# One attention and FFN kernel, its instruction order searched anew: slack behind every DMA, the first batch's k in single PSUM banks, part of v on GpSimd, other token tiles, the last tile by column halves

## The chip, the cores and the metric

The kernel runs on one core of one Trainium2 chip. The core has five engines that run their own instruction streams and wait for each other by semaphores: TensorE (PE, matmuls; PEld is its weight load), VectorE (DVE), ScalarE (ACT), GpSimd (POOL) and SyncE (SP, which here only issues DMAs). The metric is the device time in microseconds (us) of one execution; smaller is better. The profile is of one execution and covers its span, from the first instruction to the last.

## The reference

Linear attention with an exponential feature map in 8 batches of 8 heads, 576 tokens and head size 64, and then a feed-forward network (FFN) with squared ReLU on all 4608 tokens.

```python
def phi(x):
    proj = np.einsum('bhsd,df->bhsf', x, w_phi)              # 64 -> 128
    proj = proj - np.max(np.abs(proj), axis=-1, keepdims=True)
    return np.concatenate([np.exp(proj), np.exp(-proj)], axis=-1)
q_p, k_p = (phi(q), phi(k))
kv = np.einsum('bhsf,bhsd->bhfd', k_p, v)
z = np.sum(k_p, axis=2)
num = np.einsum('bhsf,bhfd->bhsd', q_p, kv)
den = np.einsum('bhsf,bhf->bhs', q_p, z)[..., None] + 1e-06
attn_out = num / den
x = attn_out.transpose(0, 2, 1, 3).reshape(4608, 512)
h = np.maximum(x @ w_in, 0.0)                                # 512 -> 2048
out = h * h @ w_out                                          # 2048 -> 512
```

All inputs and the output are float32 in DRAM; the kernel computes its matmuls in bfloat16.

## The kernel before

**Loads.** POOL issues all loads of q, k, v, w_in (`win`, four tiles of 512 KB) and w_out (`wout`, four tiles); they are cast to bfloat16 on the way. A batch of k, q or v is 512 tokens in one or more DMAs of 128 to 512 KB (`load`, line 446, and `load_q`, line 465) and a tail of 64 tokens in two small ones (line 454). SP issues the stores of the output (line 926) and the DMA transposes: of batches 2 to 7 the whole k and q into `kT` and `qT` (line 532, 18 blocks of 128x128), and of batches 1 to 7 the attention's result `xo` into `xT` (line 793), since the FFN needs it with features on partitions. In batches 0 and 1 PE transposes k and q itself (line 519, copied out of PSUM in lines 524 and 526), and in batch 0 also `xo` (line 782).

**Attention of a batch.** k comes in five groups: 0 to 3 of four 128-token blocks and 4 for the tail. `kgroup_ops` projects a group by w_phi (line 548) into a pair of PSUM banks, one for each half e of the partitions; the matmuls are 64 rows deep, two at a time on the two halves of PE. DVE takes the largest magnitude (`mk`, line 567), then ACT takes both exponentials of the pair (`kp` and `kn`, line 576, 1024 columns each). The subtraction of the maximum is not made on k: `em_ops` takes exp(-mk) and exp(mk) (lines 588 and 595), and `v_ops` multiplies v by them into `va` (DVE, lines 610 and 614, two products for each group or pair of groups). `kv_ops` sums kp with va (lines 628 and 633), and ACT copies the result to `kv` (line 642). q is projected twice: with tokens on partitions for the maxima (`qmax_ops`, lines 548 and 660, DVE 667, and `en` = exp(-2 mq), ACT 674) and with features on partitions for the exponentials (`q_ops`, PE 702, ACT 717). `out_ops` makes the numerators and denominators: matmuls NA, a product by `en` on DVE (line 744), matmuls NB on top (line 732), then reciprocal (752) and product (756) into `xo`.

**FFN.** The 4608 tokens are nine chunks of 512. Chunk 0 is done in sixteen groups of 16 matmuls of 128 columns (`ffn_in_small`, line 885), so that it can begin with the first 128 tokens. Chunks 1 to 8 are done by `ffn_in` in sixteen groups of four 512-column matmuls (line 874), each followed by ReLU on ACT (857) and the square on DVE (863). `ffn_out` (line 912) takes sixteen groups of four 512-column matmuls for each chunk, four groups to a tile of 128 tokens, then ACT copies the tile to `ot` (line 920) and SP stores it. Chunks are consecutive in blocks of 64 tokens: `blk_of` gives nine blocks to a batch, so chunk c takes blocks 8c to 8c+7, which lie in two batches. Batches with odd numbers have their tail in front, those with even numbers at the end. `xT` has three buffers for the chunks.

**The order.** All of this is first recorded in `Plan` as operations, each with an engine, an assumed cost, a due time (`key`) and what it reads and writes. `Machine` then plays the operations on a model of the engines, the PSUM banks and the DMA queues, and so fixes the order of the instructions of each engine; the instructions are written out in that order and pinned to it. An engine takes the ready operation with the earliest key. The keys come from a few constants in `K` and, for batches 0 and 1, from a table of single keys, `K["B"]`. `LIM` limits the open PSUM buffers of a kind (`tp` transposes, `att` attention pairs, and so on). An operation with a `release` time also waits for an ACT instruction that the model has finished by then; in this way loads are held back. A DMA's end in the model is its transfer and a fixed time after it:

```python
def dma_settle(t):
    for at, o in self.dma_advance(t):
        o.done = at + (SW_OUT if o.eng == "POOL" else HW_OUT)
```

While PE would have nothing to do in the first 23 us of the model, filler matmuls on a tile of zeros (`warm`, line 991) are put in.

Of the kernel before, what the change touches and what calls it, by code (L numbers as in the profile page):

```python
# [20 lines left out]
SW_IN, SW_OUT, HW_IN, HW_OUT = 1.5, 1.3, 0.75, 0.95  # L21
BEGIN = {"POOL": 1.25}
# [3 lines left out]
def act_cost(n):  # L26
    return n / 1200 + 0.050, n / 1200 + 0.165 + SEM
# [10 lines left out]
class Op:  # L38
    __slots__ = ("eng", "occ", "lat", "key", "fn", "opens", "closes", "dma", "tiled", "release", "gate",
                 "succ", "n", "ready", "at", "seq", "what", "ins", "left", "done")  # L40

    def __init__(self, eng, cost, key, fn, opens, closes, dma, tiled, release, seq, what):
        self.eng, (self.occ, self.lat), self.key, self.fn = eng, cost, key, fn
        self.opens, self.closes, self.dma, self.seq, self.what = opens, closes, dma, seq, what
        self.tiled, self.release, self.gate, self.ins = tiled, release, None, None
        self.succ, self.n, self.ready, self.at, self.done = {}, 0, 0.0, None, None

# [47 lines left out]
class Machine:  # L95
# [34 lines left out]


# [24 lines left out]
    def run(self):  # L156
# [28 lines left out]
        def dma_settle(t):  # L185
            for at, o in self.dma_advance(t):
                o.done = at + (SW_OUT if o.eng == "POOL" else HW_OUT)
                for s in o.succ:
                    released(s, o.done)
                post(o.done, o.eng)  # L190
# [6 lines left out]
        def pick(name, e, t):  # L197
# [7 lines left out]
            if mode:  # L205
                for i, op in enumerate(A):
                    if op.tiled and op.key <= t + self.ahead:
                        b = self.place(op.opens, t + 1e-9)
                        if b is not None:
                            op.opens.base = b  # L210
                            return A.pop(i)
# [4 lines left out]
            for i, op in enumerate(A):  # L216
                if op.tiled and not go and t < op.key + self.patience:
                    if op.key <= t:
                        tight = True
                    if fallback is None and self.place(op.opens, t + 1e-9) is not None:  # L220
                        fallback = i
                    continue
                if op.opens is not None:
                    b = self.place(op.opens, t + 1e-9, tight and op.opens.size == 1)
                    if b is None:
                        if op.key <= t:
                            tight = True
                        continue
                    op.opens.base = b
                return A.pop(i)  # L230
            if fallback is not None:
                op = A.pop(fallback)
                op.opens.base = self.place(op.opens, t + 1e-9)
# [3 lines left out]
        while left:  # L237
# [47 lines left out]
            if op.opens is not None:  # L285
                g = op.opens
# [22 lines left out]
def kernel(  # L309
# [67 lines left out]
    NQP = 3  # L377
    qp, qn = ring("qp", NQP, [8 * P]), ring("qn", NQP, [8 * P])
    xo = ring("xo", 3, [8 * D])
    rden = ring("rden", 3, [8], F32)  # L380
    xT = [ring(f"xT{c}", 2, [4, 2, P]) for c in range(3)]
    hr = ring("hr", 4, [TCH])
    h2 = [ring(f"h2{c}_", 4, [4, TCH]) for c in range(2)]
    ot = ring("ot", 3, [DM], F32)

# [21 lines left out]


# [16 lines left out]
    add("DVE", dve_cost(32), -20, f_warm, w=["warm"], what="warm")  # L425

    for b in range(2):
        for sg in range(2):
            def fn(b=b, sg=sg):
                pin(nc.vector.memset(va[b][sg][:, 32:40, :], 0.0))  # L430
            add("DVE", dve_cost(260), -11 if b == 0 else 0.0, fn, w=[("ve", b, sg, 4)], what="zero")
# [9 lines left out]
    def load(src, dst, b, key, tag, prs=((0, 4),), single=True, release=0.0):  # L441

        x = dst[b % 2]
        for a, z in prs:
            def fn(a=a, z=z):
# [4 lines left out]
                dma=(LD["main"] * (z - a) / 4, SW_IN, "ld"), release=release, what=tag)  # L450
        if single:
            for hi in range(2):
# [4 lines left out]
                ladd(b, (0.72, 0), key + 0.01, fn, w=[(tag, b % 2, "s", hi)], dma=(LD["s"], SW_IN, "ld"),  # L457
                    release=release, what=tag + "s")

    def load_q(b, key, jjs=(0, 1), single=True, release=0.0):  # L460

        x = xq[b % 2]
        for jj in jjs:
# [4 lines left out]
            ladd(b, (0.72, 0), key, fn, w=[("xq", b % 2, jj)], dma=(LD["main"] / 2, SW_IN, "ld"), release=release, what="xq")  # L468
        if single:
            load(q, xq, b, key, "xq", prs=(), release=release)  # L470

# [3 lines left out]
    def load_win(i, key):  # L475
# [3 lines left out]
        ladd(None, (0.72, 0), key, fn, w=[("win", i)], dma=(LD["w"], SW_IN, "ld"), what="win")  # L479

    def load_wout(i, key):
# [3 lines left out]
        ladd(None, (0.72, 0), key, fn, w=[("wout", i)], dma=(LD["w"], SW_IN, "ld"), what="wout")  # L485
# [7 lines left out]
    def blk_of(b, c):  # L493

        if c == 4:
            return b * NB + (0 if b % 2 else 8)
        return b * NB + (1 if b % 2 else 0) + 2 * c

    def attention(b):
        s2 = b % 2  # L500
        pe_in = b in PE_IN
        pe_x = b in PE_X
# [552 lines left out]
```

## Time and profile before

| What | us |
|---|---|
| median of 3 runs (lowest, highest) | 378.27 (376.19, 507.98) |
| the profiled execution's own time | 377.19 |
| its span | 375.4 |

| Group (line, engine) | count | mean ns | busy us |
|---|---|---|---|
| FFN-out matmuls, 512 columns (912, PE) | 536 of 576 recorded | 379 | 137.7 |
| FFN-in matmuls, 512 columns (874, PE) | 512 | 382 | 130.3 |
| ReLU, 512 columns (857, ACT) | 144 | 602 | 85.2 |
| square, 512 columns (863, DVE) | 144 | 418 | 59.3 |
| exponentials of k, 1024 columns, kp and kn (576, ACT) | 64 | 1020 and 1029 | 32.5 and 32.9 |
| exponentials of k, 512 columns, kp and kn (576, ACT) | 16 | 596 and 586 | 4.8 and 4.7 |
| maxima of k, 1024 columns (567, DVE) | 32 | 1216 | 38.6 |
| maxima of k, 512 columns (567, DVE) | 8 | 685 | 5.5 |
| products with v, 512 columns (610, DVE) | 16 | 688 | 10.8 |

| DMA | count | KB each | median us from issue to landing |
|---|---|---|---|
| store of a tile | 32 | 256 | 2.3 |
| store of half a tile | 8 | 128 | 2.8 |
| transpose of xo into xT | 50 | | 2.4 |
| transpose of a batch's k, q | 6, 6 | | 4.8, 5.8 |
| load of v, of k | 8, 7 | 512 | 6.4, 8.4 |
| load of win, of wout | 4, 4 | 512 | 12.0, 14.2 |

A matmul's mean is its latency, not its share of PE: successive matmuls overlap, and a group of four wide ones takes less than four times its mean. In the table "busy" is the union of the instructions' times. "Idle before" in the profile is time in which an engine had nothing, and what ended it is named after the arrow. A line of the chain of waits, "start, us, what", is a piece of the path that ended last, followed back from the end.

### The profile page before, as it was taken

How to read it: one execution, taken by the hardware profiler on the slowest of the kernel's cores; microseconds unless marked ns; L12 is line 12 of the kernel's file. 1: busy time of each engine (PE TensorE's matmuls, PEld its weight loads, DVE VectorE, ACT ScalarE, POOL GpSimd, SP SyncE). 2: the span in 40 equal slices, each digit the busy share in tenths (PEclk: the TensorE clock that was granted, in tenths of full speed). 3: DMA queues.
4: the chain of work that ended last, by engine and by line, in shares of the span. 5: the costliest groups of instructions: out<-in, count | busy, mean ns of one | idle time of the engine just before them, and what ended most of it. 6: DMA issues, size and time to landing. Idle time of an engine off the chain costs nothing.

```text
span 375.4 us, 8607 instructions
## 1 busy us (share of the span) xinstructions
PE 353.5 (94%) x3459; PEld 200.2 (53%) x3499; DVE 250.1 (67%) x417; ACT 270.1 (72%) x504; POOL 66.3 (18%) x96
## 2 busy tenths in 40 slices
PE   8997899968999999999999988999899999999995
PEld 7876768624554555455455544554445544444442
DVE  4888798883888877887678685876688762222200
ACT  2988998786798868889678977777889774444321
POOL 8634161052002500250016000610000000000000
PEclk9999999998999999999999999999999999999999
DMA  8999999699934992399519932995120222001022
GB/s 94 195 200 204 149 112 148 122 119 141 137 71 91 146 192 64 59 152 205 86 48 129 203 73 73 115 196 111 43 71 9 47 61 70 30 28 56 30 58 82
DMA packets 101799, 39.62 MB, mean 106 GB/s; under 512 B 76544, under 2 KB 97152, under 8 KB 101760
## 3 DMA queue, kind: packets, MB, share of 16 engines
q0 software_dynamic: 50592, 18.36, 43.4%
q1 hardware_dynamic: 51168, 20.72, 25.0%
q8 instruction: 27, 0.44, 0.5%
q14 instruction: 12, 0.10, 0.1%
HBM read 36.77 MB, written 9.44 MB: 123 GB/s over the span
## 4 chain that ended last, share of the span: by engine, by line
PE 70%; ACT 13%; DVE 7%; DMA 6%; issue 3%; ACTq 0%; DVEq 0%; SPq 0%; POOLq 0%
PE psum L912 25%; PE psum L874 24%; PE psum L732 5%; DMA xT<-xo 4%; PE psum L548 4%; ACT kn L576 4%; ACT hr L857 3%; PE psum L628 3%; PE psum L885 3%; ACT kp L576 3%; PE psum L702 2%; DVE va L614 2%; DVE mk L567 2%; DMA xk<-in_k_dram 1%; PE psum L991 1%
## 5 line engine op out<-in xcount | busy, mean ns | idle before, releaser
L912 PE MATMUL psum<-wout,h 128*128 128x512 bf16 x536 | 137.7, 379 | 2.8 <-issue 1.1
L874 PE MATMUL psum<-xT,win 128*128 128x512 bf16 x512 | 130.3, 382 | 7.9 <-DMA xT<-xo 7.7
L857 ACT ACTIVATE hr<-psum 128x512 bf16<-128x512 f32 x144 | 85.2, 602 | 58.4 <-PE psum L874 56.0
L863 DVE TENSOR_TENSOR h<-hr 128x512 bf16<-128x512 bf16 x144 | 59.3, 418 | 60.6 <-ACT hr L857 59.8
L912 PEld LDWEIGHTS <-h 128*128 128x128 bf16 x576 | 52.2, 98 | 56.5 <-issue 0.2
L874 PEld LDWEIGHTS <-win 128*128 128x128 bf16 x512 | 47.7, 98 | 63.8 <-issue 7.6
L667 DVE TENSOR_REDUCE mq<-psum 128x8 f32<-128x1024 f32 (+1 forms) x40 | 44.3, 1112 | 3.7 <-PE psum L548 2.0
L567 DVE TENSOR_REDUCE mk<-psum 128x8 f32<-128x1024 f32 (+1 forms) x40 | 43.9, 1109 | 2.6 <-PE psum L548 2.2
L614 DVE TENSOR_TENSOR va<-xv,va 128x1024 bf16<-128x1024 bf16 (+1 forms) x36 | 38.5, 1104 | 7.4 <-ACT va L595 7.4
L576 ACT ACTIVATE kp<-psum 128x1024 bf16<-128x1024 f32 (+1 forms) x40 | 37.2, 936 | 6.9 <-DVE mk L567 6.8
L717 ACT ACTIVATE qp<-psum 128x1024 bf16<-128x1024 f32 (+1 forms) x40 | 37.0, 937 | 3.4 <-PE psum L702 2.8
L744 DVE TENSOR_TENSOR psum<-psum,en 128x520 f32<-128x520 f32 (+1 forms) x40 | 27.8, 701 | 16.2 <-PE psum L732 13.8
L576 ACT ACTIVATE kn<-psum 128x1024 bf16<-128x1024 f32 (+1 forms) x40 | 37.6, 941 | 0.0
L717 ACT ACTIVATE qn<-psum 128x1024 bf16<-128x1024 f32 (+1 forms) x40 | 37.6, 945 | 0.0
L920 ACT ACTIVATE ot<-psum 128x512 f32<-128x512 f32 x36 | 21.6, 601 | 17.2 <-PE psum L912 17.1
L446 POOL DMA_DIRECT2D xv<-in_v_dram x8 | 7.2, 900 | 138.5 <-ACT hr L857 63.8
L756 DVE TENSOR_TENSOR xo<-psum,rden 128x512 bf16<-128x512 f32 (+1 forms) x40 | 27.2, 684 | 0.9
L628 PE MATMUL psum<-va,kp 128*128 128x65 bf16 x256 | 20.0, 194 | 0.8 <-ACT kv L642 0.7
L628 PE MATMUL psum<-va,kn 128*128 128x65 bf16 x256 | 19.9, 193 | 0.1
L628 PEld LDWEIGHTS <-kp 128*128 128x128 bf16 x256 | 17.4, 97 | 4.3 <-issue 2.0
L732 PEld LDWEIGHTS <-qp 128*128 128x128 bf16 x320 | 14.7, 97 | 7.7 <-issue 0.5
L628 PEld LDWEIGHTS <-kn 128*128 128x128 bf16 x256 | 16.8, 97 | 3.2 <-issue 1.5
(54 smaller groups left out, 347.0 us busy)
## 6 DMA issues: line engine op xcount, KB each, us to landing
out_dram<-ot SPq DMA_DIRECT2D x32, 256.0 KB, 2.3
xq<-in_q_dram POOLq DMA_DIRECT2D x16, 256.0 KB, 5.6
xv<-in_v_dram POOLq DMA_DIRECT2D x8, 512.0 KB, 6.4
xk<-in_k_dram POOLq DMA_DIRECT2D x7, 512.0 KB, 8.4
win<-in_moe_w_in_dram POOLq DMA_DIRECT2D x4, 512.0 KB, 12.0
wout<-in_moe_w_out_dram POOLq DMA_DIRECT2D x4, 512.0 KB, 14.2
out_dram<-ot SPq DMA_DIRECT2D x8, 128.0 KB, 2.8
xT<-xo SPq DMA_TRANSPOSE x50, 2.4
```

Of the source, the lines that this page charges most:

```text
L567: pin(nc.vector.tensor_reduce(out=mk_view(g), in_=ps2(pj)[:, :, : n * Fd].rearrange("p e (i f) -> p e i f", f=Fd), axis=AX.X, op=ALU.max, ...
L576: pin(nc.scalar.activation(out=dst[slot][:, :, :n, :].rearrange("p e i f -> p e (i f)"), in_=ps2(pj)[:, :, : n * Fd], func=ACT.Exp, scale= ...
L614: pin(nc.vector.tensor_tensor(out=o[:, :, :D], in0=xv[s2][:, 512 * g0 : 512 * g1].rearrange("p (m d) -> p m d", d=D), in1=o[:, :, D].to_br ...
L628: pin(nc.tensor.matmul(out=o[:, sg, hi, :], lhsT=(kp, kn)[sg][kgroup[pr]][:, j % 2, 2 * hi + j // 2, :], rhs=va[s2][sg][:, 8 * pr + 4 * hi ...
L667: pin(nc.vector.tensor_reduce(out=mqb[:, c, :, :n], in_=ps2(pj)[:, :, : n * Fd].rearrange("p e (i f) -> p e i f", f=Fd), axis=AX.X, op=ALU ...
L717: pin(nc.scalar.activation(out=o, in_=i_, func=ACT.Exp, scale=sgn))
L732: pin(nc.tensor.matmul(out=o[:, u // 4, u % 4 * D1 : (u % 4 + 1) * D1], lhsT=(qp, qn)[sg][slot][:, u * m : u * m + P], rhs=kv_sb[s2][:, h ...
L744: pin(nc.vector.tensor_tensor(out=o, in0=o, in1=enb[:m, c, :].rearrange("t (b h) -> t b h", b=2).to_broadcast([m, 2, 4, D1]), op=ALU.mult))
L857: pin(nc.scalar.activation(out=hr[sl], in_=ps1(g), func=ACT.Relu))
L863: pin(nc.vector.tensor_tensor(out=dst, in0=i_, in1=i_, op=ALU.mult))
L874: pin(nc.tensor.matmul(out=o, lhsT=win[mc // 4][:, kc, mc % 4 * P : (mc % 4 + 1) * P], rhs=xT[c % 3][kc // 2][:, :, kc % 2, :], start=(kc ...
L912: pin(nc.tensor.matmul(out=ps1(g), lhsT=h2[c % 2][mc // 4][:, mc % 4, tt * P : (tt + 1) * P], rhs=wout[mc // 4][:, mc % 4, :], start=(mc = ...
```

## The change

The computation is the same. These parts differ:

- **Model.** A DMA's end in the model gets a further time, by kind (`SLACK`: 0.4 us for the first loads and weights, 1.5 us for later loads and for transposes of `xo`, 2.5 us for transposes of k and q). An operation may open several PSUM buffers at once (`fit`). ACT's cost has a floor.
- **Order.** Every operation gets a key of its own from a list `KEYS` (one number for each operation, in hundredths of a microsecond), and every held-back load a release time from a list `RELEASES`. The limits become `tp` 6, `b0` 7, `att` 3, `kv` 1, `op` 2; `hp` has none.
- **First batch's k.** `kgroup_ops` opens two single banks for a group, one for each e, instead of a pair. Maxima and exponentials are by bank, half as wide and twice as many: maximum of e=0, exponentials of e=1, exponentials of e=0, maximum of e=1, of which each pair on different banks may run at once.
- **First batch's v.** Three of the ten products go to GpSimd (`CV`: group 0 and group 1 one each, tail one).
- **Copies out of PSUM** of the transposed k and q in batches 0 and 1 are given to ACT or DVE one by one (`CK`, `CQ`, `CK1`, `CQ1`); in batch 1 all ten were on ACT, now four are.
- **Token tiles.** Chunk b, for b from 0 to 7, is the first 512 tokens of batch b; chunk 8 is the eight tails, gathered in a buffer `xS`. `xT` has two buffers instead of three. A batch after the first has four DMA transposes of 128 tokens into `xT` and one of 64 into `xS`; before there were 50 in all, now 35.
- **Last tile.** `last_out` computes tile 3 of chunk 8 in two PSUM banks, 256 columns each, copies one half by ACT and one by DVE, and stores each half in two DMAs, one issued by SP and one by ACT. The three other tiles of chunk 8 are stored in two DMAs of 64 tokens each.
- `load_v0` and the values `KM` = 2 are written for further variants; with `KM` all 1 they load v as before.

The diff, cut:

```diff
+SLACK = {"first": 0.4, "ld": 1.5, "x": 1.5, "kq": 2.5}
...
-                o.done = at + (SW_OUT if o.eng == "POOL" else HW_OUT)
+                o.done = at + (SW_OUT if o.eng == "POOL" else HW_OUT) + o.slack
...
+    def fit(self, op, t, tight=False):
+
+        got = []
+        for g in op.opens:
+            b = self.place(g, t, tight and g.size == 1)
+            if b is None:
+                break
+            got.append((g, b, self.free_at[b : b + g.size]))
+            self.free_at[b : b + g.size] = [1e9] * g.size
+        for g, b, was in got:
+            self.free_at[b : b + g.size] = was
+        if len(got) < len(op.opens):
+            return False
+        for g, b, was in got:
+            g.base = b
+        return True
...
-    xT = [ring(f"xT{c}", 2, [4, 2, P]) for c in range(3)]
+    xT = [ring(f"xT{c}", 2, [4, 2, P]) for c in range(NXT)]
+    xS = sb("xS", [4, KC, P])
...
+            if first and KM[g]:
+
+                pj = [Bank(1, "b0"), Bank(1, "b0")]
+                def fn():
+                    for i, t in enumerate(ts):
+                        for e in range(2):
+                            r = slice(64 * e, 64 * e + 64)
+                            pin(nc.tensor.matmul(out=ps1(pj[e])[:, i * Fd : (i + 1) * Fd], lhsT=kTb[r, t, :],
+                                                 rhs=wphi2[r, :], start=True, stop=True))
...
+                def maxes(e, last):
+                    def fn():
+                        pin(nc.vector.tensor_reduce(
+                            out=mk_view(g)[:, e, :], in_=ps1(pj[e])[:, : n * Fd].rearrange("p (i f) -> p i f", f=Fd),
+                            axis=AX.X, op=ALU.max, apply_absolute_value=True))
...
+                        def fn(dst=dst, sgn=sgn):
+                            pin(nc.scalar.activation(out=dst[slot][:, e, :n, :].rearrange("p i f -> p (i f)"),
+                                                     in_=ps1(pj[e])[:, : n * Fd], func=ACT.Exp, scale=sgn))
...
+                maxes(0, False)
...
+                    exps(1, False)
+                    exps(0, True)
+                    maxes(1, True)
...
-                def fn(sg=sg):
+                on = K["CV"][2 * g0 + sg] if first else "DVE"
+                ve = nc.vector if on == "DVE" else nc.gpsimd
...
+                    pin(nc.sync.dma_start_transpose(out=o, in_=xo[xs][:m, :]))
+                add("SP", (1.23, 0), key, fn, r=[("xo", xs)], w=toks, dma=(0.8 * m / P, HW_IN, "x", "x"), what="Xx")
...
-            qorder = [4, 0, 1, 2, 3] if b % 2 else [0, 1, 2, 3, 4]
+            qorder = [0, 1, 2, 3, 4]
...
+    def x_toks(c, ts):
+        if c == NCH - 1:
+            return [("xS", b) for b in range(B)]
+        return [("xT", c % NXT, t, hh) for t in ts for hh in range(2)]
...
+        for half in range(2):
+            add("PE", pe_cost(4, 0.109), key + half * (2.0 if part == 3 else 0.01), mm(half),
+                r=[("wout", part)] + [("h2", c % 2, 4 * part + i, tt) for i in range(4)],
+                w=[gs[half]], opens=gs[half] if part == 0 else None, what="F2h")
...
+        if (c, tt) == (NCH - 1, 3):
+            last_out(c, tt, part, key)
+            return
...
+    for op, key in zip(plan.ops, KEYS):
+        op.key = key / 100
+    for op, at in zip([op for op in plan.ops if op.release > 0], RELEASES):
+        op.release = at / 100
...
+    'CV': ['POOL', 'DVE', 'DVE', 'POOL', 'DVE', 'DVE', 'DVE', 'DVE', 'DVE', 'POOL'],
+    'KM': [1, 1, 1, 1, 1],
+    'CK': ['DVE', 'ACT', 'ACT', 'DVE', 'DVE'],
+    'CQ': ['DVE', 'DVE', 'DVE', 'ACT', 'ACT'],
+    'CK1': ['ACT', 'ACT', 'ACT', 'ACT', 'DVE'],
+    'CQ1': ['DVE', 'DVE', 'DVE', 'DVE', 'DVE'],
...
+    'LIM': {'tp': 6, 'b0': 7, 'att': 3, 'kv': 1, 'op': 2},
```

## The prediction

> **What bounds the kernel now.** I read the engine shares first, then the windows by stage, then the waits, and last the chain of waits and the queues at the places that these name.
>
> ```profile
> PE 353.5 (94%) x3459; PEld 200.2 (53%) x3499; DVE 250.1 (67%) x417; ACT 270.1 (72%) x504; POOL 66.3 (18%) x96
> ```
>
> TensorE is the bound on average, but the average hides the stages. The windows are cut at the first FFN matmul (35.2), the first wide FFN-in (81.2) and the last attention matmul (302.4); columns are PE, PEld, DVE, ACT, POOL, clock, DMA:
>
> ```profile
> 0.00:35.20 35.20, 31.25 (x460) 25.92 (x461) 24.74 (x40) 24.22 (x46) 20.79 (x34) 1.00 1.25 171
> 35.20:60.00 24.80, 22.59 (x373) 18.14 (x371) 21.07 (x39) 23.89 (x51) 9.04 (x13) 1.00 1.19 147
> 60.00:81.20 21.20, 20.62 (x272) 13.59 (x273) 19.52 (x35) 17.24 (x31) 3.03 (x5) 1.00 0.71 107
> 81.20:85.64 4.44, 0.59 (x3) 0.10 (x1) 1.81 (x2) 1.50 (x2) 2.14 (x4) 0.93 1.41 228
> 85.64:226.14 140.50, 136.67 (x1322) 72.39 (x1339) 109.18 (x176) 114.58 (x218) 24.03 (x33) 0.99 0.81 118
> 226.14:302.40 76.26, 73.24 (x700) 38.48 (x712) 57.31 (x91) 59.81 (x110) 7.29 (x10) 1.00 0.51 83
> 302.40:371.30 68.90, 68.53 (x339) 31.61 (x346) 16.44 (x38) 28.26 (x47) 0.00 (x0) 1.00 0.16 51
> 371.30:375.40 4.10, 0.02 (x1) 0.00 (x0) 0.00 (x0) 0.60 (x1) 0.00 (x0) 0.97 0.18 66
> ```
>
> Up to 35.2 the PE's busy time is mostly warm-up filler; ACT is the real limit (next fence). From 35.2 to 60 ACT is full (23.89 of 24.8). From 302.4 to 371.3 PE has no gap; nothing can be gained there. In between stands one class of wait, on DMA transposes (engine, tile, waited for: us, times, longest; then the chain):
>
> ```profile
> PE psum L874 <- DMA xT<-xo: 7.7, 4, 3.9
> ```
>
> ```profile
> 78.06 7.54 DMA xT<-xo
> ...
> 223.76 2.33 DMA xT<-xo
> ...
> 259.35 4.24 DMA xT<-xo
> ...
> 299.92 2.34 DMA xT<-xo
> ...
> 320.38 0.86 PE psum L912 x4
> ```
>
> The SP queue shows why: both 18-block transposes of the next batch go ahead of six small ones that the FFN waits for.
>
> ```profile
> 208.61 4.22 SPq L532 DMA_TRANSPOSE qT<-xq  x1
> 212.92 0.54 SPq L926 DMA_DIRECT2D out_dram<-ot  x1
> 213.62 2.83 SPq L532 DMA_TRANSPOSE kT<-xk  x1
> 218.37 7.88 SPq L793 DMA_TRANSPOSE xT<-xo  x6
> ```
>
> And the start of ACT:
>
> ```profile
> 6.97 1.28 ACT L526 ACT_TABLE_LOAD   x1 [6.97 <-DVE kT L524]
> 8.72 0.60 ACT L526 ACTIVATE kT<-psum 128x512 bf16<-128x512 bf16 x1 [0.46 <-PE psum L519]
> ...
> 9.56 1.01 ACT L576 ACTIVATE kp<-psum 128x1024 bf16<-128x1024 f32 x1
> ```
>
> The table load sits behind a wait on DVE, so it is paid while the first k already lies there.
>
> **PE work does not change.** Both kernels have the same FFN, attention and transposition matmuls (one 512-column tile becomes two of 256), and the order of the changed kernel switches PE in and out of the 64-row projections 120 times, before 124; after the first wide FFN-in 78 times in both. A group of four 512-column matmuls takes 0.86 us back to back (last line of the chain above). From 85.64 to 226.14 I count 254 FFN-in and 51x4 FFN-out matmuls at 0.216 us, 99.0 us, and 3.85 attentions in the other 41.5 us, 10.8 each. So only waits can go. The sum is against the profiled execution: span 375.4, its own time 377.19, 1.8 more; the median 378.27 is 1.1 above that, and the highest, 507.98, is left aside.
>
> **1. Start of ACT: -2.5.** In the new order the table load waits for nothing. The first load is 128 KB, not 256 KB (landing 3.9 and 4.5 us): 1.25 + 3.9 = 5.2, then 0.64 for four transposes (5.82 to the copy at 6.46), 0.60 copy, 0.54 projection: first exponential at 7.1, not 9.56. With e=0 and e=1 in banks of their own, it no longer stands behind the 1.22 us maximum. If the load lands as late as before, -1.5.
>
> **2. ACT up to the last copy of kv (30.0 to 30.3 before): -2.0.** Before: 14 wide exponentials (0.91 apart), 2 narrow and 3 copies (0.49), 11 small ones and 4 `en` (2.1 in all), 4 kv copies (0.27): 18.4 us of work in 20.7. After: 16 half-width exponentials at 0.49 and 4 at 0.27 (8.9; the split costs 0.7), 4 q exponentials (3.6; two have moved behind), one copy each of 0.49 and 0.27, the small ones 2.2, kv copies 1.1: 16.6. With the same 12% of gaps 18.7, so 2.0 less. Both steps together bring the first FFN matmul to about 30.7. They hold only while ACT is the limit. DVE has 14.5 us in the same stretch: maxima 5.5, seven v products 4.2, six copies 2.5, two q maxima 2.3. Loads cover too: 1.4 MB lie ahead of the last k tile, 7 us at 200 GB/s, landed at about 11, needed at 14. The second half of q has moved behind the first win tile: 1.9 MB, landed at some 14 to 18, its projections come near 20. The last win tile is issued behind 3.4 MB and lands by 24, for FFN matmuls at 30. If that cover is gone, nothing is left of step 2.
>
> **3. Three v products on GpSimd: 0.** They free 1.8 us of DVE (0.60 each), which has room. Their own time has no near row: POOL's only arithmetic is the 0.26 and 0.35 us of `ident`. Scaled from 128 to 512 columns that is 1.0 to 1.4 us. The Trainium skill's GPSIMD Engine Reference (3.1, Elementwise) has 2.6 cycles per element, an estimate of 1.1. A rule speaks against it: SBUF — State Buffer (Summary: rules for kernel authors) says that a DVE instruction with two SBUF inputs and a GpSimd instruction that reads SBUF exclude each other, the later waiting in full. A v product is just that. The row at hand, 0.69 us of the v product, is alone on the port and can't test it. By the row the step gives up to -1; by the rule DVE loses 3 x 1.1 - 1.8 = +1.5. I take 0, as DVE isn't the limit. These three also stand in POOL's queue ahead of batch 1's k and q, all of wout and batch 1's v; cover is the eight DMAs in flight, three of them win at 512 KB, 7.5 us. Past that each us moves wout, which I place at 42 against a need at about 47.
>
> **4. From the first FFN matmul to the first wide FFN-in (46 us): -2.** ACT is full to 60. The copies of batch 1's kT and qT were all ACT's; now four kT copies are, and one kT and all five qT are DVE's: 5 x 0.49 + 0.27 = 2.7 off ACT, 2.3 onto DVE (21.1 of 24.8 before, so it has 3.7). Bounds: 0, if DVE becomes the limit there, and -4.
>
> **5. Waits on transposes: -6.5 of 7.7.** Chunk c is now the first 512 tokens of batch c, and the tails go into `xS` for the end. SP issues 35 such transposes instead of 50, per batch four of 1.2 us and a small one. Needed after the last numerator matmul: reciprocal and `xo` 0.9, perhaps one transpose ahead 1.2, landing 2.4: 4.5. The PE work that the new order puts between is, for chunks 1 to 7, 5.2, 6.4, 9.3, 5.4, 5.8, 5.8 and 5.8 us (3 to 8 FFN groups at 0.86 and attention pieces at 0.3). Before, at 226, it was 3.8. Chunk 5 now needs eight of nine blocks of batch 5, before three; these numbers already pay for it. The 7.54 us at 78 ran into batch 3's v and q, issued from 76.5 to 82; in the new order such 512 KB loads are tied to ACT instructions after the first FFN-in, or well ahead. I leave 1.2, since slack is thin at chunks 1 and 4. Bounds: -7.7, and 0.
>
> **6. Rest of the middle: -1.** PSUM limits change (six transposition banks may be open, not one) and the keys are all new; PE idles only 6.9 us in the two windows from 85.64 to 302.4, and 3.8 of it are waits of step 5 (7.7 less the 3.9 ahead of 85.64). Bounds +2, if the new order stalls more often, and -4 (10.2 per attention).
>
> **7. End: +0.5.** The tile in column halves isn't last: the new order puts another tile's sixteen 512-column matmuls behind it. That one goes out in one 0.6 us copy and two 128 KB stores (landing 2.8) instead of one of 256 KB (2.3). Bounds 0 and +1.
>
> Removed filler matmuls, DVE memsets and stores on ACT's queue: 0, as these engines are idle there (ACT 0.60 of the last 4.1).
>
> Sum: -2.5 -2.0 -2 -6.5 -1 +0.5 = -13.5; span 361.9, time **363.7**.
>
> **Rivals.**
>
> *A. As summed*, 359 to 368; chance 0.60. For it: ACT's start and the SP rows above.
>
> *B. All waits go and attention comes to 10.2*: another -1.2 and -3 to -4, to 358.5, with a start at 29 some 357; 0.15. Against it: the count of switches is the same.
>
> *C. Waits stay in another place*: step 5 gives nothing, because loads or stores stand ahead of the transposes: 363.7 + 6.5 = 370.2; 0.22. For it: landing of the same transpose runs from 2.4 to 7.5.
>
> *D. Slower, by the SP queue.* SP runs in order, and stores that wait for ACT's `ot` stand between the four transposes of batches 3 to 7. If every chunk's last transpose takes 7.5 us as at 78, it needs 0.9 + 1.2 + 7.5 = 9.6 against about 6.2: 3.3 us for each of seven chunks, 23, in place of 7.7. Then 363.7 - 1.2 + 23 = 385.5. It decides from 2.3 us per chunk on (7 x 2.3 brings 362.5 to 378.6). Against it: only one of the waits before was of that size. 0.03.
>
> *The change doesn't do what it says* holds for the last tile; it is in the sum.
>
> **How the numbers follow.** The likeliest case gives 363.7. Range 356 to 371: B and the lower bounds of steps 4 to 6 below, C with a lost step 3 above; about one in ten is left out, mostly beyond C. Within 2% means above 370.7: a little under half of C, so 0.09; D is slower, 0.03; the rest, 0.88, is faster.
>
> **What would show it.** Right: no `xT<-xo` in PE's waits above 1 us; the table load before 3 us; the first FFN matmul between 29 and 32; a gapless PE at the end; two stores after the last copy. Wrong: GpSimd products beyond 2 us or DVE products stretched beside them (step 3), a wait of FFN-out on wout (POOL's queue), an `xT` wait at chunks 1 or 4 (C), or at all seven (D).

## The result and the profile after

| | us |
|---|---|
| changed kernel, median of 4 runs (lowest, highest) | 371.6 (371.12, 372.21) |
| kernel before, beside it, median of 4 (lowest, highest) | 377.58 (376.19, 507.98) |
| ratio after to before, with its 95% interval | 0.9854 [0.9815, 0.9894] |
| forecast | 363.7 (356 to 371) |
| the profiled execution's own time, its span | 372.21, 370.4 |

The kernel is 1.5% faster, not 3.8%, and 0.6 us above the forecast range. A ratio, here and below, is of fast runs alone: a run more than 1.5% above the fastest of its kernel, as the one of 507.98, counts in the median and not in the ratio. The sum of the forecast was -13.5 us on the span of 375.4; the span fell by 5.0. Engine shares of the changed kernel:

```profile
PE 349.5 (94%) x3458; PEld 199.8 (54%) x3494; DVE 254.9 (69%) x426; ACT 267.8 (72%) x507; POOL 69.7 (19%) x99
```

Busy time by stage, cut at the same events as before (first FFN matmul, 60, first wide FFN-in, behind the wait there, last weight load; the wait itself ended at 83.02); columns are PE, PEld, DVE, ACT, POOL, clock, DMA share, GB/s:

```profile
0.00:34.90 34.90, 28.57 (x414) 23.97 (x415) 24.91 (x42) 23.49 (x55) 25.52 (x38) 0.95 1.25 156
34.90:60.00 25.10, 23.72 (x388) 19.72 (x387) 23.32 (x47) 22.59 (x43) 6.37 (x9) 1.00 1.07 147
60.00:80.90 20.90, 19.91 (x272) 12.72 (x275) 16.18 (x25) 13.66 (x27) 3.37 (x5) 1.00 1.08 136
80.90:84.60 3.70, 2.18 (x23) 0.98 (x20) 2.09 (x4) 2.84 (x6) 0.00 (x0) 1.00 0.59 167
84.60:365.20 280.60, 274.66 (x2379) 142.45 (x2407) 188.44 (x312) 204.67 (x378) 34.44 (x47) 1.00 0.61 95
365.20:370.40 5.20, 0.46 (x3) 0.00 (x0) 0.00 (x0) 0.60 (x1) 0.00 (x0) 0.82 0.22 50
```

The first row ends where the first row of before ended, at about 35: 4.5 us were to be saved there, and only 0.3 are. The wait ahead of the first wide FFN-in shrank from 3.9 to 1.5 us. What PE waits for now:

```profile
PE psum L992 <- DMA xT<-xo: 2.2, 3, 1.5
PE psum L569 <- DVE mq L781: 1.8, 1, 1.8
PE psum L569 <- POOL ident masks.py:199: 1.2, 1, 1.2
PE psum L992 <- ACT hr L972: 1.1, 1, 1.1
```

The first row was 7.7. The other three stand in no row of the kernel before; where the third stands now, PE there waited 0.7 us for the first k. The chain of waits shows what is left of the first:

```profile
65.02 8.42 DMA xk<-in_k_dram
73.46 5.84 DMA kT<-xk
79.40 3.58 DMA xT<-xo
...
155.30 7.44 DMA xT<-xo
```

A last k tail of batch 2, issued at 65, lands 8.4 us later and holds the transposition of k, and that holds chunk 1's. At 155 a transposition that takes 2.3 us at best lands after 7.4.

To see where the 5.0 us came from, I took the starts of all weight loads and subtracted, stretch by stretch, the spacing that each kind of matmul has back to back; what is left is PE's time without work. Fillers count as time without work. The change from before to after: +0.6 us up to the first FFN matmul, -1.3 from there to the first wide FFN-in, -2.5 at the wait there, -2.6 in all that follows, and +0.8 behind the last weight load (from it to the end 4.7 us before, 5.4 after). In the first stretch 0.9 us of PE's work has moved behind the first FFN matmul, so that this matmul comes 0.3 us earlier although the time without work grew.

### The profile page after: what moved, and what is told of

Same layout as the page of the kernel before. It is cut to its first block, busy times and chain, and to the rows that moved or that the text cites. A ratio compares the mean times of both kernels' runs of the same rounds, so it can differ in the third digit from the quotient of the medians.

```text
span 370.4 us, 8515 instructions
## 1 busy us (share of the span) xinstructions
PE 349.5 (94%) x3458; PEld 199.8 (54%) x3494; DVE 254.9 (69%) x426; ACT 267.8 (72%) x507; POOL 69.7 (19%) x99
## 4 chain that ended last, share of the span: by engine, by line
PE 57%; ACT 18%; DMA 9%; issue 7%; DVE 6%; POOL 2%; POOLq 0%; DVEq 0%; ACTq 0%
PE psum L992 21%; PE psum L1057 21%; ACT hr L972 5%; PE psum L846 4%; DMA xT<-xo 4%; PE psum L741 3%; ACT kp L684 3%; ACT kn L684 2%; DMA xk<-in_k_dram 2%; PE psum L598 2%; ACT qp L831 2%; PE psum L816 2%; DMA kT<-xk 2%; DVE mq L781 2%; ACT ot L1065 1%
## 5 line engine op out<-in xcount | busy, mean ns | idle before, releaser
L1057 PE MATMUL psum<-wout,h 128*128 128x512 bf16 x524 | 128.2, 379 | 3.2 <-issue 1.1
L992 PE MATMUL psum<-xT,win 128*128 128x512 bf16 x448 | 104.3, 379 | 4.0 <-DMA xT<-xo 2.2
L972 ACT ACTIVATE hr<-psum 128x512 bf16<-128x512 f32 x144 | 83.0, 607 | 28.8 <-PE psum L992 18.5
L1057 PEld LDWEIGHTS <-h 128*128 128x128 bf16 x560 | 50.2, 98 | 53.7 <-issue 2.3
L1065 ACT ACTIVATE ot<-psum 128x512 f32<-128x512 f32 x35 | 21.0, 601 | 29.3 <-PE psum L1057 21.5
L678 DVE TENSOR_REDUCE mk<-psum 128x8 f32<-128x1024 f32 (+1 forms) x35 | 38.0, 1109 | 3.5 <-PE psum L598 3.1
L684 ACT ACTIVATE kp<-psum 128x1024 bf16<-128x1024 f32 (+1 forms) x35 | 32.8, 939 | 6.8 <-DVE mk L678 6.6
L684 ACT ACTIVATE kn<-psum 128x1024 bf16<-128x1024 f32 (+1 forms) x35 | 33.0, 944 | 0.1
L487 POOL DMA_DIRECT2D xq<-in_q_dram x16 | 14.2, 888 | 39.7 <-ACT va L703 13.8
L476 POOL DMA_DIRECT2D xk<-in_k_dram x16 | 10.1, 629 | 52.9 <-DVE mq L781 19.7
```

What stands on the lines that cost most here:

```text
L678: pin(nc.vector.tensor_reduce(out=mk_view(g), in_=ps2(pj)[:, :, : n * Fd].rearrange("p e (i f) -> p e i f", f=Fd), axis=AX.X, op=ALU.max, ...
L684: pin(nc.scalar.activation(out=dst[slot][:, :, :n, :].rearrange("p e i f -> p e (i f)"), in_=ps2(pj)[:, :, : n * Fd], func=ACT.Exp, scale= ...
L972: pin(nc.scalar.activation(out=hr[sl], in_=ps1(g), func=ACT.Relu))
L992: pin(nc.tensor.matmul(out=o, lhsT=win[mc // 4][:, kc, mc % 4 * P : (mc % 4 + 1) * P], rhs=x, start=(kc == 0), stop=(kc == KC - 1)))
L1057: pin(nc.tensor.matmul(out=ps1(g), lhsT=h2[c % 2][mc // 4][:, mc % 4, tt * P : (tt + 1) * P], rhs=wout[mc // 4][:, mc % 4, :], start=(mc = ...
```

## The experiments

The edits leave the order that the planner found: outside each edit the traces list the same instructions in the same order. The table has the median, the ratio to the kernel before with its interval, and from the one profiled execution of each the starts of the first exponential and of the fourth copy of kv, and the first FFN matmul (in us).

| kernel | median | ratio | exp | kv | FFN |
|---|---|---|---|---|---|
| before | | 1 | 9.56 | 30.01 | 34.99 |
| changed | 371.60 | 0.9854 [0.9815, 0.9894] | 8.22 | 28.98 | 34.69 |
| a2_after (the same) | 372.67 | 0.9888 [0.9864, 0.9912] | 7.39 | 28.16 | 34.21 |
| e1_v_dve | 369.33 | 0.9794 [0.9722, 0.9866] | 7.37 | 26.74 | 32.94 |
| e2_ident | 372.70 | 0.9857 [0.9790, 0.9924] | 6.16 | 28.70 | 34.85 |
| e3_v_ident | 372.90 | 0.9873 [0.9819, 0.9927] | 6.78 | 27.69 | 34.00 |
| e4_loads | 371.14 | 0.9846 [0.9770, 0.9921] | 7.35 | 28.98 | 34.70 |
| e5_tail | 372.94 | 0.9802 [0.9720, 0.9884] | 7.36 | 27.07 | 33.11 |
| e6_v6_pool | 370.85 | 0.9823 [0.9777, 0.9869] | 7.36 | 25.98 | 32.33 |
| e9_v_narrow | 370.49 | 0.9829 [0.9776, 0.9882] | 7.36 | 25.20 | 31.41 |
| b1_before_v_pool | 377.04 | 1.0010 [0.9990, 1.0030] | 9.02 | 28.85 | 33.82 |
| e7_three | 369.74 | 0.9815 [0.9789, 0.9842] | 7.36 | 26.49 | 32.69 |
| e10_fill | 379.59 | 1.0092 [1.0059, 1.0126] | 7.36 | 28.45 | 36.83 |
| e8_all | 377.89 | 0.9991 [0.9966, 1.0015] | 7.37 | 26.57 | 34.95 |
| c1_six | 371.98 | 0.9837 [0.9800, 0.9873] | 8.19 | 30.43 | 36.64 |
| c2_fill | 371.42 | 0.9839 [0.9821, 0.9856] | 7.43 | 26.92 | 32.96 |
| c3_copies | 372.54 | 0.9885 [0.9857, 0.9912] | 8.25 | 27.80 | 33.51 |

### v back on DVE (e1_v_dve)

```diff
-                ve = nc.vector if on == "DVE" else nc.gpsimd
+                ve = nc.vector
```

> The changed kernel with its three GpSimd v products put back on DVE, at the same places of the order; nothing else moves. Theory (the two engines exclude each other on these products): all v products take 0.69 us on DVE again, none 1.5; PE's wait of 1.84 us on DVE's mq ahead of the transposition at 23.2 goes, the half-clock stretch of 3.4 us goes with it, the first FFN matmul comes at 31.5 to 32.5 instead of 34.7, and the time falls by 2 to 3 us (ratio to the kernel before 0.977 to 0.980). Rival (DVE is simply full there): three more products of 0.69 us on DVE keep mq as late as it was, the first FFN matmul stays within 0.5 us of 34.7, time unchanged.

In the changed kernel, DVE's and then GpSimd's timeline (start, us, engine, line, operation) around 20 us:

```profile
17.64 0.68 DVE L724 TENSOR_TENSOR va<-xv,va 128x512 bf16<-128x512 bf16 x1
18.24 0.68 DVE L633 TENSOR_REDUCE mk<-psum 128x4 f32<-128x512 f32 x1
18.96 1.56 DVE L720 TENSOR_TENSOR va<-xv,va 128x512 bf16<-128x512 bf16 x1
20.45 1.54 DVE L724 TENSOR_TENSOR va<-xv,va 128x512 bf16<-128x512 bf16 x1
21.91 1.21 DVE L781 TENSOR_REDUCE mq<-psum 128x8 f32<-128x1024 f32 x1
```

```profile
18.92 1.05 POOL L720 TENSOR_TENSOR va<-xv,va 128x512 bf16<-128x512 bf16 x1 [0.33 <-ACT va L696]
19.99 1.45 POOL L724 TENSOR_TENSOR va<-xv,va 128x512 bf16<-128x512 bf16 x1
```

The same DVE product takes 0.68 us alone and 1.56 beside a GpSimd product, and its end lies 0.55 us behind the end of that product both times (19.97 to 20.52, 21.44 to 21.99): it has waited it out. In e1_v_dve the same four products are all on DVE:

```profile
18.23 1.29 DVE L720 TENSOR_TENSOR va<-xv,va 128x512 bf16<-128x512 bf16 x2
19.44 1.29 DVE L724 TENSOR_TENSOR va<-xv,va 128x512 bf16<-128x512 bf16 x2
```

Each of the ten took 0.68 to 0.69, the wait for mq went from 1.8 to 0.8 us, and the first FFN matmul came at 32.94, later than the 31.5 to 32.5 expected. A stretch at half clock did not vanish; it moved from 23.8 to 29.3. The time is 2.3 us lower, but the intervals overlap.

### The identity earlier (e2_ident, e3_v_ident)

```diff
+    ident_op = [o for o in order if o.what == "ident"][0]
+    order.remove(ident_op)
+    order.insert([i for i, o in enumerate(order) if o.what == "xk"][0] + 1, ident_op)
```

> The changed kernel with the identity matrix built on GpSimd right behind the first k load instead of behind four loads. Theory (the first transposition waits for it): the wait of 1.17 us on GpSimd goes, the first transposition starts at about 5.2 instead of 5.86 and the first exponential at 7.5 instead of 8.2; if ACT sets the end of the start, the time falls by 0.5 to 0.7. Rival (the stretch around 20 to 27 us, with DVE late and the clock halved, sets it): the first exponential comes earlier just the same, but the first FFN matmul and the time stay within 0.3 us.

> Both edits together: v products all on DVE and the identity early. Theory: the sum of the two, first FFN matmul at about 31 to 31.5, time 2.5 to 3.5 us below the changed kernel, because with the stretch on DVE gone ACT is the limit and its earlier start is passed on in full. Rival: no more than the larger of the two alone.

The rival holds for both. In e2 the first exponential came 2.1 us earlier (6.16; 0.85 of it is the clock of the first ten us, see the last section), the first FFN matmul did not (34.85), nor did the time fall; the other loads, now behind the identity in POOL's queue, cost PE a new wait of 1.4 us for k at 7.5. In e3 PE waits 2.0 us for the first half of q, which lands at 13.2; in e1 it waits 1.0 for it (12.3), and in the changed kernel, at half clock, not at all. ACT's early start is not what the end of this stage hangs on: loads and then DVE hold it up.

### Less work on DVE (e9_v_narrow)

```diff
-                            out=o[:, :, :D], in0=xv[s2][:, 512 * g0 : 512 * g1].rearrange("p (m d) -> p m d", d=D),
-                            in1=o[:, :, D].to_broadcast([P, 8 * (g1 - g0), D]), op=ALU.mult))
+                            out=o[:, :, :dw], in0=xv[s2][:, 512 * g0 : 512 * g1].rearrange("p (m d) -> p m d", d=D)[:, :, :dw],
+                            in1=o[:, :, D].to_broadcast([P, 8 * (g1 - g0), dw]), op=ALU.mult))
```

(`dw` is 1 in batch 0, so that the kernel leaves out 63 of 64 columns of v in eight of the ten products; all ten are on DVE. Not shown: the rest of `va` is filled with zeros ahead, by one more DVE memset and one ACT copy.)

> All v products of batch 0 on DVE, and eight of them (all but the two of the tail) cut to one of 64 columns; the rest of v is filled with zeros ahead of time, so that part of batch 0's result is left out. DVE loses some 4.5 us of work between 10 and 26, all waits stay. Theory (DVE, not ACT, is the limit of the start once v is on it): the first FFN matmul comes 2 to 3 us before the 32.9 that it has with full products on DVE, at 30 to 31, where ACT's work alone had put it. Rival (ACT or the loads are the limit, as the forecast had it): first FFN matmul within 0.5 us of 32.9.

The eight products took 0.18 to 0.20 us, and the fourth kv copy started at 25.20, the first FFN matmul at 31.41: 1.5 us before the same kernel with whole products (e1), between the two expectations and nearer the theory. DVE's work holds the kv copies up. It is not the only limit: 4 us of work taken off bring 1.5, and the chain of waits then runs over the load of the second half of q instead of over DVE:

```profile
13.09 6.77 DMA xq<-in_q_dram
19.90 0.40 PE psum L573 x4
```

In the changed kernel the chain runs over ACT from 10.7 us to 18.9, and then over DVE:

```profile
18.62 0.32 ACT va L696 x2
18.96 1.56 DVE va L720
20.52 1.47 DVE va L724
21.99 1.14 DVE mq L781
23.13 0.04 issue
23.18 0.38 PE psum L569 x4
```

The windows from the first maximum of k to the end of the fourth maximum of q agree, of the kernel before and of the changed one:

```profile
8.20:29.10 20.90, 19.61 (x295) 15.73 (x294) 17.64 (x23) 18.38 (x39) 10.46 (x15) 1.00 1.41 194
```

```profile
8.26:29.57 21.31, 19.28 (x296) 15.84 (x295) 18.86 (x27) 16.98 (x45) 15.74 (x21) 0.92 1.37 168
```

ACT (fourth column of work) fell from 18.4 to 17.0 us, as forecast. DVE rose from 17.6 to 18.9 in 21.3 us: apart from PE, whose time holds fillers, it took over as the fullest engine, and it was nearly so before.

### Six products on GpSimd, and three in the kernel before (e6_v6_pool, c1_six, b1_before_v_pool)

```diff
+                ve = nc.gpsimd if first and (g0, sg) in ((0, 0), (0, 1), (1, 1), (2, 1), (3, 0), (4, 1)) else nc.vector
```

> The changed kernel with six of the ten first v products on GpSimd instead of three; all else stays. Theory (exclusion): DVE products that meet a GpSimd product take 1.3 to 1.6 us instead of 0.69, the first FFN matmul comes 1.5 to 3 us later than 34.7, at 36 to 38, and the time is 1.5 to 3 us above the changed kernel's. Rival (no exclusion, DVE is relieved of three more): the first FFN matmul comes 1 to 2 us earlier, at about 33.

> The kernel before with the same three v products moved to GpSimd, nothing else. Theory (exclusion): the DVE products beside them are stretched to about 1.5 us and the move is no gain: first FFN matmul between 35.0 and 37, time the same to 2 us above the kernel before. Rival (DVE is relieved): first FFN matmul 0.5 to 1 us earlier than 35.0, time 0.5 to 1 us lower.

> The three edits with six of ten v products on GpSimd in place of none. Theory A (exclusion makes GpSimd products a loss): 0.5 to 1.5 us above the three edits' 369.7. Theory B (a GpSimd product costs DVE at most what it takes off it, and where the two do not meet it is a gain): 0.5 to 1.0 us below 369.7, first FFN matmul near 32.3.

The expectation of e6 failed: the first FFN matmul came at 32.33, the earliest with whole products. But c1_six, which has the same six products and the same instructions up to there, had it at 36.64, the latest without fillers of its own. DVE and GpSimd there:

```profile
18.93 4.70 DVE L720 TENSOR_TENSOR va<-xv,va 128x512 bf16<-128x512 bf16 x1
23.54 1.21 DVE L781 TENSOR_REDUCE mq<-psum 128x8 f32<-128x1024 f32 x1
```

```profile
18.77 0.80 POOL L534 DMA_DIRECT2D win<-in_moe_w_in_dram  x1
19.53 1.12 POOL L720 TENSOR_TENSOR va<-xv,va 128x512 bf16<-128x512 bf16 x1
20.55 2.12 POOL L724 TENSOR_TENSOR va<-xv,va 128x512 bf16<-128x512 bf16 x2
```

One DVE product stood behind three GpSimd products in a row: 4.70 us, and PE waited 3.0 us for it. Its record starts 0.6 us before the first of them; what held it until then is not shown. In e6 the same one took 1.56, and 1.1 of that lie before GpSimd's first product there, so that its stretch is not explained either. In e4 one DVE product waited out two in a row (2.73 us), while in the changed kernel DVE's came in between the two. So GpSimd products are no fixed price but a draw, a matter of how the instructions happen to meet: where they miss DVE's products they relieve it, where they meet they hold it for one product of GpSimd or for several. The medians can't tell the price: c1's ratio, 0.9837, and that of the same edits with all products on DVE (e7), 0.9815, have intervals that overlap.

In the kernel before, three of them stretched one DVE product (1.55 us). The first FFN matmul came 1.2 us earlier there (33.82), as the rival had it, and still the time stayed where it was, 1.001 [0.999, 1.003].

For three on GpSimd, six profiled executions (changed, a2, e2, e4, e5, c3) have the first FFN matmul at 34.2 on average; for none, four (e1, e3, e7, c2) have it at 33.1. About 1 us goes with the move here, over a spread of 1.7. It isn't shown to be DVE's alone: the three latest of the six (changed, e2, e4: 34.7 to 34.9) are those with a stretch at half clock that begins at 24 to 25 us, and the other three (33.1 to 34.2) have none there.

### Batch 2's loads earlier (e4_loads)

```diff
+    lead = [o for o in order if o.seq == 372][0]
+    for o in [o for s in (368, 365, 366) for o in order if o.seq == s][::-1]:
+        order.remove(o)
+        o.gate = lead.gate
+        order.insert(order.index(lead) + 1, o)
```

> The changed kernel with three loads of batch 2 (second half of q, k, one k tail) issued right behind batch 2's v load at about 49.5 instead of from 57 to 65. Theory (these loads come late, so their transpositions stand on SP ahead of chunk 1's): the wait of 1.5 us on xT at 83.0 and the 0.7 us on kT ahead of it go, first wide FFN-in at about 79, time 1.5 to 2.5 us lower. Rival (SP's own order is the limit, the transposition of q holding SP for 7.5 us wherever it stands): the wait moves by less than 0.5 us and the time stays.

The transposition of q, which SP issues at 63.14 in the changed kernel, goes out at 58.68, and the waits between 78 and 90 us are, in the changed kernel and here:

```profile
PE psum L992 <- DMA xT<-xo: 1.5, 1, 1.5
PE psum L598 <- DMA kT<-xk: 0.7, 1, 0.7
```

```profile
PE psum L992 <- ACT hr L972: 1.6, 2, 1.2
```

Both waits on DMAs are gone; from the first FFN matmul to chunk 1's first FFN-out it is 1.7 us shorter (66.1 to 64.4). By the last weight load 0.8 of that is left: behind 90 us PE waits more than in the changed kernel, for transpositions into xT 1.3 us against 0.7, for a copy of ACT 0.9 against 0.6. The mechanism is the theory's; the median moved by 0.5, and its runs lie from 370.6 to 374.4.

### The tile in halves really last (e5_tail)

```diff
+    for n, o in enumerate(o for o in plan.ops if o.what == "F2h"):
+        o.key = 600.0 + n % 2 * 10 + n
```

> The changed kernel with the tile in column halves made the last on PE, as its name says (first one half's sixteen matmuls, then the other's). Theory (the end is the copy and the stores of the last tile): the last copy is of 256 columns, on ACT and DVE by halves, its stores of 64 KB on two queues, so the time from the last weight load to the end falls from 5.4 to 4.7 us or less, time 0.5 to 0.8 us lower. Rival (fixed cost of a store and of the end of the program): the tail stays within 0.2 us of 5.4.

Last weight load to end: 4.4 us (365.6 to 370.0), without the edit 5.4. The last copy is now one of 256 columns:

```profile
362.49 3.51 PE psum L1021 x32
...
366.09 0.42 DVE otl L1035
```

The tail's gain of 1.0 us is drowned in the median by its runs, which lie from 368.5 to 376.4.

### Once more, and the three edits together (a2_after, e7_three)

> The changed kernel once more, unedited, for its spread. Theory (its start hangs on where the half-clock stretches of TensorE fall): the runs differ by up to 3 us, in steps of about 1.2 us for each stretch of 3.4 us at half clock that the mean granted clock shows (0.9955, 0.991, 0.9865 for one, two, three); median 371 to 373. Rival (its runs agree as those of a kernel with fixed waits would): all runs within 1 us of 371.6.

> Three of the single edits together: v products on DVE, batch 2's loads right behind its v, the column-halves tile last. From the single runs' stages: 0 to 1.5 us in the start, 1.7 us between the first FFN matmul and the second chunk, 1.0 us in the tail. Theory (they lie on different stages and add): 2.7 to 4 us below the changed kernel, 367.5 to 369. Rival (the gain of the middle is given back at the next chunk's waits, as the load edit alone lost 0.9 of its 1.7 us by the end): 1.5 to 2.5 us below.

The changed kernel's six runs lie within 1.7 us; steps in the granted clock are there (0.998 with 371.47, 0.989 with 373.13), but are smaller than expected. The three edits (v on DVE, batch 2's loads, tail) bring 369.74 against 372.67 on the same chip, 2.9 us less, and their intervals do not touch. That is in the range of a full sum, 2.7 to 4, but the runs of both are too wide apart to exclude the rival's 2.5. This is the version that beats both kernels.

### Fillers (e10_fill, c2_fill), and a load moved (e8_all)

```diff
+                    for _ in range(10 if first and c in (0, 1, 2) else 0):
+                        pin(nc.tensor.matmul(out=o[:, 0, 384:512], lhsT=warm, rhs=warm, start=(sg == 0), stop=(sg == 0), skip_group_check=True))
...
+            n += {63: 10, 112: 12}.get(op.seq, 0)
```

(c2_fill has the three edits and only the 10 fillers at operation 63, the first transposition. e8_all has the three edits, all fillers, and batch 5's v load moved in front of a k load at about 165.)

> The changed kernel with more filler matmuls where TensorE waits in the start: 10 more ahead of the first transposition, 12 ahead of the one that waits for DVE at 21 us, and 10 ahead of each half of the first three numerators of batch 0. Theory (waits of 1 to 2 us cost a stretch of 3.4 us at half clock each): no half-clock stretch between 10 and 34 us, first FFN matmul 0.7 to 1.5 us earlier on average than in the changed kernel, time 1 to 1.5 us lower and its spread under 2 us. Rival (TensorE waits anyway in these stretches, so that its clock does not matter): half-clock stretches go, the time stays within 0.5 us, or rises by the 0.6 us that a filler group takes.

> The three edits, the fillers, and batch 5's v load (512 KB) moved from 151 us to about 164, behind chunk 3's transpositions. Theory: the last transposition of chunk 3 lands in about 3 us instead of 7.4, the wait of 0.9 to 1.1 us on xT ahead of chunk 3 goes, and with the fillers the time is 1.5 to 2.5 us below that of the three edits alone, 365.5 to 367. Rival (the landing is slow because of batch 4's v load issued in front of it): the wait stays, and the time is within 1 us of the three edits.

> The three edits with 10 more filler matmuls ahead of the first transposition, nowhere else. Theory A (the half clock of the first ten us costs time): every run starts at full clock, the median falls by 0.5 to 1 us and the spread (2.6 us for the three edits) to under 2. Theory B (DVE sets the start from 11 us on, and the early half-clock stretch is hidden by it): median within 0.3 us of 369.7.

e10 has no stretch at half clock up to 206 us, yet its first FFN matmul came 2 us later. Its fillers write the numerators' own bank, so they stood behind the wait that they were to fill:

```profile
30.86 0.72 PE L845 MATMUL psum<-warm 128*128 128x128 bf16 x10 [0.80 <-DVE psum L860]
31.41 0.42 PE L848 MATMUL psum<-kv,qn 128*128 128x65 bf16 x8
32.85 0.72 PE L845 MATMUL psum<-warm 128*128 128x128 bf16 x10 [1.02 <-DVE xo L872]
```

That is a fault of the edit, so it does not show what the clock alone costs there (the last section has one measure of it). Later waits grew as well (3.3 us at chunk 4); why was not tried. In c2 the fillers stand ahead of the wait for the identity and cost nothing there: the clock was full from 4.0 to 31.3 us, and the first FFN matmul is where it was (32.96). But e1 and e7 had the full clock there without these fillers (first exponential 7.37), so that c2 doesn't test whether the half clock of the first ten us is hidden. Its median, on another chip than e7's, fits neither expectation; its ratio, 0.9839, can't be told from e7's 0.9815, and its profile has a wait of 2.6 us on xT at chunk 3.

In e8 the wait at chunk 3 went, as expected, and chunk 4 got a larger one:

```profile
204.15 2.10 PE L994 MATMUL psum<-xT,win 128*128 128x512 bf16 x9 [2.68 <-DMA xT<-xo]
```

Its two last transpositions went out at 195.10 and 197.23 and had landed 9.0 us after the first, beside loads issued from 193 to 202; in e7 it was 6.8. The moved load is not shown to have spoiled this chunk: e10, with the same fillers and that load in its old place, waited 3.3 us at the same chunk. The profiled execution is 6.1 us longer than that of e7, 2.3 up to the first FFN matmul and 3.8 behind 89 us; what of it the fillers cost and what the load stays open.

### Batch 1's copies back on ACT (c3_copies)

```diff
-                if eng == "DVE":
+                if eng == "DVE" and b == 0:
```

> The changed kernel with the copies of batch 1's five q blocks and one k block put back on ACT, as in the kernel before. Theory (step 4 of the forecast: ACT is full from 35 to 60): from the first FFN matmul to the first wide FFN-in it takes 1.5 to 2.5 us longer than the 46.2 of the changed kernel, time 1 to 2.5 us above 372. Rival (that stretch is set by loads and transpositions, not by ACT): within 0.5 us of 46.2 and of 372.

From the first FFN matmul to the first wide FFN-in: 47.45 us against 46.2, between the two expectations. PE's time without work there is 6.7 us, as in the kernel before (6.8), against 5.4. So the copies on DVE are worth some 1.25 us in their stretch by these two executions; the fourteen profiled ones with the copies on DVE take from 45.4 to 47.25 us there (e6 the longest), so the size isn't certain. And the wait for xT behind it falls from 1.5 to 0.7 us, and the time, 372.5, is that of a2: while that wait stands, most of what is gained ahead of it is only waited off.

## Why the forecast missed

| step | forecast | measured, change of PE's time without work |
|---|---|---|
| 1, 2, 3: start of ACT, ACT up to kv, products on GpSimd | -4.5 | +0.6 |
| 4: up to the first wide FFN-in | -2 | -1.3 |
| 5, 6: waits on transposes, rest of the middle | -7.5 | -5.1 |
| 7: end | +0.5 | +0.8 |
| sum | -13.5 | -5.0 |

**The step that failed is step 2**, and step 1 with it. Its ACT side was right: 17.0 us of work against 16.6 forecast, with the table load at 0.74. It said "They hold only while ACT is the limit" and gave DVE 14.5 us of work. In the changed kernel's timeline DVE has 20.2 us in that stretch when its instructions are added up (18.9 without their overlaps): ten k maxima 6.3 (5.5 forecast), seven v products 6.5 (4.2), copies 2.5 (as forecast), and four q maxima 4.9 (2.3 for two, though two more stand in DVE's order ahead of the first product of the numerators). And its room is not ACT's 20.7 us: it begins with the first maximum and ends with the last. The row of the kernel before already had DVE at 17.64 of 20.9, and the prediction's own first row has DVE at 24.74 against ACT's 24.22. e9 takes the work off and gets the kv copies at the 25 to 26 us that step 2 needs; e2 starts ACT earlier and gets nothing. The loads were later than step 2 placed them, too: the second half of q landed at 20.4 us (forecast 14 to 18), the last win tile at 29.6 (by 24); with DVE's work off, that half of q is the next in the chain. Step 1 came to 8.22 for the first exponential instead of 7.1: the sum left out the identity matrix, for which PE's first transposition waited 1.2 us, and the eleven fillers behind it took 1.38 us at half clock instead of 0.78 (last section). What remains between e9's 31.4 and the forecast of 30.7 is behind the last kv copy: 5.3 to 6.0 us from its end to the first FFN matmul in these orders, 4.6 before, of which the forecast took the latter.

**Step 3** weighed the rule of the Trainium skill (SBUF — State Buffer, Summary: rules for kernel authors) against a row that could not test it, and took 0. The trace agrees with the rule that one waits for the other, 1.56 against 0.68 us, but not that it is always the later one: in e4 and c1 the DVE product whose record starts first is the one that waits. The mean start puts its price at about +1 us in this kernel, inside the bounds of -1 and +1.5, with the clock's share in it not separated. GpSimd's own time, 1.05 us where undisturbed, was as estimated.

**Step 4** had the right mechanism, with its size 1.3 for 2 and not certain (c3). The bound that it named, DVE at its limit, was near: from 34.9 to 60 DVE is now busy 23.32 us of 25.10, more than ACT (22.59). **Step 5** too: its own row fell by 5.5 us of the 6.5 forecast, and slack was thin where it said, at chunk 1. The k tail's late load was not in the sum; e4 shows it. **Step 6** was to bring -1 and brought nothing (-5.1 in all, of which the row of step 5 has 5.5): PE gained a wait of 1.1 us at 89 us for ACT's ReLU, in every profile of this order (ACT is busy 18.05 of 19 us from 81 to 100). **Step 7** was right, and the reason too: with the halves last the tail is 4.4 us instead of 5.4.

Rival C, with waits left in another place, came near in time (370.2), but by luck, for a reason that it did not name: it left them at the transposes, and the larger part was lost ahead of the first FFN matmul.

## What to carry to other kernels

When work is moved off the fullest engine, count the next engine's work over its own room, from its first possible instruction to its last, and by the rows of the same window; a stage has two engines near full more often than one. Products with two SBUF inputs on GpSimd beside such products on DVE are a draw, not a relief: put them where DVE has none, or leave them. A gain ahead of a wait that still stands is waited off there, so small edits are best judged together.

## What the runs showed of the hardware

Of 71 runs of the kernel before, 63 fall into three groups by the mean granted clock: 0.995 with a mean of 376.5 us (32 runs), 0.991 with 377.5 (23), 0.986 with 379.3 (8). One stretch of 3.41 us at half clock in 375 is 0.0045 of the mean, so each further stretch goes with 1 to 2 us.

One stretch can be priced by a pair of executions. The changed kernel and c3_copies have the same instructions up to 39 us. The changed kernel's profile has half clock from 23.83 to 27.25, that of c3 has none from 10 us on to beyond its first FFN matmul. From the transposition that waits for mq to the first FFN matmul it is 11.5 us in the one (23.18 to 34.69) and 10.5 in the other (22.97 to 33.51): 1.0 us.

The clock column reads 1.00 up to 10 us in the profile of the changed kernel, but the trace has no clock record there, and the matmuls say otherwise. The same eleven fillers in the changed kernel and in e1_v_dve:

```profile
6.24 1.38 PE L1144 MATMUL psum<-warm 128*128 128x128 bf16 x11
```

```profile
6.05 0.78 PE L1144 MATMUL psum<-warm 128*128 128x128 bf16 x11
```

1.38 us against 0.78, in two executions whose instructions are the same up to there. Which of the two an execution gets changes the first exponential by 0.85 us. In one pair it did not change the first FFN matmul (34.69 and 34.70 in the changed kernel and e4_loads); whether it decides how DVE's and GpSimd's products meet (e6 began at full clock, c1 at half) was not tried.
